# Norm factors of a fused retention and expert kernel: spread over the partitions through DRAM instead of by products with ones

## The chip, the cores and the metric

The kernel runs on one core of a Trainium2 chip. The metric is the device time of one execution in microseconds (us). A core has a matrix engine (PE, TensorE), a vector engine (DVE), a scalar engine (ACT), GpSimd (POOL) and SyncE (SP), which here only issues DMA transfers. Each engine takes its instructions in the order in which they were written, and waits on semaphores for the others.

## What is computed

Three layers follow each other on 2304 tokens (4 batches of 576) of 512 features:

```python
x = retention(q, k, v)                       # per batch and head, with decay
rms = np.sqrt(np.mean(x * x, axis=-1, keepdims=True) + 1e-06)
xn = x / rms * rms_g                         # one factor per token
x = (silu(xn @ w_gate) * (xn @ w_val)) @ w_out
out = sum over 8 experts of P[:, e] * (relu(x @ w1[e]) @ w2[e])
```

The change concerns `1 / rms`, one number per token. The kernel holds x with the features on the partitions and the tokens along the free axis. So a token's factor is needed in all 128 partitions, in the column of that token.

## The kernel before

The program is written with a manual schedule: the order of the Python calls is the order on every engine, and generators (`next(...)`) interleave the pieces of work.

The first stage is the retention loop over `i` in 0 to 15, four head pairs for each of four batches. Step `i` issues on SP the loads of `qT` and `vs` for `i + 2`; then PE makes `scores(i + 1)` (tile `sc`) and `states(i + 1)` (tile `u`), DVE multiplies `sc` by the masks into `am` (L293) and scans the states (L313, L314); SP issues `kT` and `ks` for `i + 3`; and PE makes `outputs(i)` (tile `o`), which DVE scales into `acc` (L342, L344), ACT squares (L349) and POOL adds up over the four pairs of a batch (L351). `sc` and `o` have two buffers each in PSUM; `kT` and `ks` two in SBUF, `qT` and `vs` three, so a load of step `i` waits until PE has read the buffer's last contents. SP issues every load on one queue, in the written order, the weights of the second stage too (`raw`, L109). In the same loop ACT and DVE cut the weights into two parts (L124 to L146).

The norm of batch `b` has two generators. `norm_sums(b)` sums the squares over the partitions by PE (tile `ss`), and makes the factors `r` = `ry`: 128 partitions by 5 columns, token `c * 128 + p` in partition `p`, column `c` (POOL power, then one Newton step on DVE, L385 to L387). `norm(b)` then has to bring them into a row that all partitions hold (tile `y`, 128 x 576), and multiplies x by it, pair by pair (L408); ACT rounds the result into `xhi` (L409), and DVE or POOL takes the rest into `xlo` (L412, L414). The first yields of `norm(b)` are the part that the change replaces: ACT makes five scaled identities `dg` (L395), PE multiplies them by ones into `rb` (L399, L400; the batches 2 and 3 call the second tile `rbt`), ACT copies that into `y` (L402, L403).

For batch 0 this runs in the steps i = 7 to 13 of the retention loop. Batch 1 starts there (i = 13 and 15) and goes on in the first gated block. The second stage is the gated one: six sweeps over five blocks of tokens (`gated_block`, tile `gv` for gate and value, `x` for the output). In the first sweep the norms of the batches 1, 2 and 3 are interleaved with the blocks 0, 1 and 2. The third stage holds the experts, about three quarters of the time, and is not touched.

Of the kernel before, what the change touches and what calls it, by code (L numbers as in the profile page):

```python
# [9 lines left out]
F32 = mybir.dt.float32  # L10
# [7 lines left out]
B, H, S, D = 4, 8, 576, 64  # L18
NP = H // 2
# [6 lines left out]
C = 128  # L26
NC = S // C
TAIL = S - NC * C
# [22 lines left out]
def retention_glu_experts(ctx: ExitStack, tc: tile.TileContext, a, out):  # L51
# [6 lines left out]
    nc = tc.nc  # L58
# [6 lines left out]
    kept = ctx.enter_context(tc.tile_pool(name="kept", bufs=1, space=bass.MemoryType.DRAM))  # L65
# [6 lines left out]
    ident = const.tile([128, 128], F32, name="ident")  # L72
    ones = const.tile([128, 128], F32, name="ones")
# [278 lines left out]
        squares[b] = sq  # L352
        yield

    normed, rstd = set(), {}

    def bank(name):
        pool, tag = ps_home
        return pool.tile([128, 512], F32, tag=tag, name=name)

    def two_banks(b):
        if b < 2:
            t = psa.tile([128, 2, 512], F32, tag="sc", name=f"rb{b}")
            return t[:, 0], t[:, 1]
        return bank(f"rb{b}"), bank(f"rbt{b}")

    def norm_sums(b):

        sq = squares.pop(b)
        if b < B - 1:  # L370
            ss = psa.tile([128, 2, 512], F32, tag="sc", name=f"ss{b}")[:, 0, :NC + 1]
        else:
            ss = bank(f"ss{b}")[:, :NC + 1]
        for c in range(NC + 1):
            w = C if c < NC else TAIL
            nc.tensor.matmul(ss[:w, c:c + 1], lhsT=sq[:, c * C:c * C + w], rhs=ones[:, :1], start=True, stop=True)
        v = nrm.tile([128, NC + 1], F32, tag="rv", name=f"rv{b}")
        r = nrm.tile([128, NC + 1], F32, tag=f"ry{b}", name=f"ry{b}")
        t = nrm.tile([128, NC + 1], F32, tag="rt", name=f"rt{b}")
        nc.vector.memset(v, 1.0)  # L380
        nc.vector.tensor_scalar(v[:, :NC], ss[:, :NC], 1.0 / DM, 1e-6, ALU.mult, ALU.add)
        nc.vector.tensor_scalar(v[:TAIL, NC:], ss[:TAIL, NC:NC + 1], 1.0 / DM, 1e-6, ALU.mult, ALU.add)
        nc.gpsimd.tensor_tensor(out=r, in0=v, in1=mhalf, op=ALU.pow)
        yield
        nc.vector.tensor_mul(t, r, r)  # L385
        nc.vector.scalar_tensor_tensor(t, t, -0.5, v, ALU.mult, ALU.mult)
        nc.vector.scalar_tensor_tensor(r, t, 1.5, r, ALU.add, ALU.mult)  # L387
        rstd[b] = r

    def norm(b):  # L390
        r = rstd.pop(b)
        dg = nrm.tile([128, (NC + 1) * C], F32, tag="dg", name=f"dg{b}")
        dg = dg.rearrange("p (c i) -> p c i", i=C)
        for c in range(NC + 1):
            nc.scalar.mul(dg[:, c, :], ident, r[:, c:c + 1])  # L395
        yield
        rb, rt = two_banks(b)
        rt = rt[:, :TAIL]
        nc.tensor.matmul(rb, lhsT=ones, rhs=dg[:, :NC, :], start=True, stop=True)  # L399
        nc.tensor.matmul(rt, lhsT=ones[:TAIL, :], rhs=dg[:TAIL, NC, :TAIL], start=True, stop=True)  # L400
        y = nrm.tile([128, (NC + 1) * C], F32, tag="dg", name=f"y{b}")[:, :S]
        nc.scalar.copy(y[:, :NC * C], rb)  # L402
        nc.scalar.copy(y[:, NC * C:], rt)  # L403
        yield
        ts = slice(b * S, (b + 1) * S)
        for pr in range(NP):
            x = acc_d[:, pr, ts]
            nc.vector.scalar_tensor_tensor(x, x, rms_g[:, pr:pr + 1], y, ALU.mult, ALU.mult)  # L408
            nc.scalar.copy(xhi[:, pr, ts], x)  # L409
            if pr:  # L410
                p = acc_d[:, pr - 1, ts], f32(xhi[:, pr - 1, ts])
                (nc.vector if pr % 2 else nc.gpsimd).tensor_sub(xlo[:, pr - 1, ts], *p)  # L412
            yield
        nc.vector.tensor_sub(xlo[:, pr, ts], acc_d[:, pr, ts], f32(xhi[:, pr, ts]))  # L414
        normed.add(b)
# [36 lines left out]
    for i in range(B * NP):  # L452
        b, pr = divmod(i, NP)
        load_pair(i + 2, "qT", "vs")
        load_weights(1)
        if i == 2:
            nc.sync.dma_start(rms_g, a["rms_g"])
            nc.sync.dma_start(ident, a["ident"])
            nc.sync.dma_start(wg_raw.rearrange("p k e -> p (k e)"), a["wg"])
        scores(i + 1)  # L460
        states(i + 1)
        load_pair(i + 3, "kT", "ks")
        scale_keys(i + 2)
        out_steps = outputs(i)
        next(out_steps)
        step_weights(load=False, apart=1)
        next(out_steps)
        if i in SUMS_AT:
            next(sums[i // NP - 1], None)
        if i >= 2 * NP - 1:  # L470
            next(norms[0], None)
        if i in (B * NP - 3, B * NP - 1):
            next(norms[1])
    assert 0 in normed
    retention.close()
# [148 lines left out]
    for s in range(NSWEEP):  # L624
        last_sweep = s == NSWEEP - 1
        for j, (t0, n) in enumerate(BLOCKS):
            last = j == len(BLOCKS) - 1
            block = gated_block(s, t0, n, last, pmm, pac, hp, tp, 1 if last_sweep and last else KD, 512)
            first_norms = not s and j + 1 < B
            assert s or (t0 + n - 1) // S in normed  # L630
            for i in range(2 * SWEEP + 1):
                if last_sweep and last and i == 2 * SWEEP:
                    break
                if first_norms and j and not i:
                    next(norms[j + 1])
                if i == 2 * SWEEP:
                    step_weights()
                next(block)
                if first_norms:
                    for _ in range((1, 1, 1, 2, 0)[i]):  # L640
                        next(norms[j + 1], None)
                    if not j and i in (1, 2):
                        next(sums[B - 1], None)
                    if i == 2 * SWEEP - 1 and j + 2 < B:
                        next(norms[j + 2])
                if i == 2 * SWEEP or i < 2 and not first_norms or i == 2 and not s:
                    step_weights()
                if not s and last and not i:
                    nc.scalar.copy(wg[:, :, :E], wg_raw)
                    nc.vector.tensor_sub(wg[:, :, E:], wg_raw, f32(wg[:, :, :E]))  # L650
                if last_sweep and j and i % 2:
                    next(scored)
                if last_sweep and j == 1 and i == 2:
                    load_job(0)
                    load_job2(0)
                if last_sweep and j >= 3:
                    next(first_unit, None)
                    if j == 4:
                        next(first_job, None)
            else:  # L660
                for _ in block:
                    assert 0
# [649 lines left out]
```

## Time and profile before

| what | value |
|---|---|
| time, median of 3 runs (lowest to highest) | 2000.55 us (2000.46 to 2002.4) |
| span of the profiled execution, first to last instruction | 1999.9 us |
| PE busy | 1983.4 us, 99% |
| DVE, ACT, POOL busy | 72%, 43%, 37% |
| granted TensorE clock | 1.000 on average over the span |
| share of the DMA engines in the first 50 us (slice 1 of 40) | 9 tenths |

The span is that of the profiled execution; the median of the timed runs is 0.65 us longer, which is what lies around the span. A share of busy time is an average over stages. PE is busy nearly everywhere; what it waits for in the first 86 us, the retention loop, has to be read there.

### The profile page before, as it was taken

The page shows a single profiled execution, that of the slowest core. Times are in us where ns is not written, and L with a number is a line of the kernel's source. Part 1 is how long each engine was busy: PE and PEld are TensorE (multiplying, and loading weights), DVE is VectorE, ACT ScalarE, POOL GpSimd, SP SyncE. Part 2 cuts the span into 40 slices and gives each one's busy share as a digit, 9 for nine tenths or more (in the row PEclk, how much of TensorE's full clock was granted, in tenths as well). Part 3 has the DMA queues.
Part 4 walks back from the last instruction along what each step waited for, and adds up shares of the span by engine and source line. Part 5 has one row for each costly group of instructions (what it writes and reads, how often), then busy time and mean ns, then how long its engine had stood idle before and what let it go on. Part 6 is the DMA issues. An engine that isn't in the chain of part 4 may idle for free.

```text
span 1999.9 us, 29898 instructions
## 1 busy us (share of the span) xinstructions
PE 1983.4 (99%) x11390; PEld 1856.2 (93%) x11390; DVE 1441.8 (72%) x2276; ACT 869.7 (43%) x1655; POOL 740.4 (37%) x692
## 2 busy tenths in 40 slices
PE   9999999999999999999999999999999999999998
PEld 7788988988889998999999999999999999999998
DVE  6865555554688777777786777777787777777777
ACT  4453323322454444444444444444445444444443
POOL 3300000000153544545544444545466454444543
PEclk9999999999999999999999999999999999999999
DMA  9411111110178888888888676767767767676773
GB/s 314 150 32 53 50 45 52 44 43 1 48 294 301 291 301 305 308 295 311 303 309 313 245 279 239 276 254 263 265 237 282 264 256 280 237 266 251 271 260 142
DMA packets 111535, 436.56 MB, mean 218 GB/s; under 512 B 11720, under 2 KB 29128, under 8 KB 95008
## 3 DMA queue, kind: packets, MB, share of 16 engines
q1 hardware_dynamic: 109904, 432.39, 59.5%
q8 instruction: 89, 1.46, 0.3%
q10 hardware_dynamic: 1248, 1.49, 0.2%
q0 software_dynamic: 240, 0.79, 0.1%
q14 instruction: 54, 0.44, 0.1%
HBM read 312.41 MB, written 122.21 MB: 217 GB/s over the span
## 4 chain that ended last, share of the span: by engine, by line
PE 95%; DVE 3%; DMA 1%; ACT 1%; POOL 0%; issue 0%; ACTq 0%; SPq 0%; DVEq 0%; POOLq 0%
PE py L751 10%; PE pz L751 10%; PE px L751 10%; PE qx L997 7%; PE qy L997 6%; PE qz L997 6%; PE gv L177 5%; PE gv L179 5%; PE gv L178 5%; PE y L178 4%; PE y L179 4%; PE y L177 4%; PE qz L751 3%; PE x L177 2%; PE x L178 2%; PE x L179 2%
## 5 line engine op out<-in xcount | busy, mean ns | idle before, releaser
L751 PE MATMUL py<-sx,w1s 128*128 128x384 f32 x1152 | 232.0, 335 | 1.1 <-ACT py L1089 0.9
L539 POOL TENSOR_TENSOR t<-rw 128x256 f32<-128x256 f32 x32 | 43.0, 1343 | 508.2 <-DVE sx L576 398.8
L1178 POOL TENSOR_TENSOR acc<-z,a_block 128x384 f32<-128x384 f32 x63 | 64.0, 1015 | 434.7 <-DVE z L1172 434.7
L751 PEld LDWEIGHTS py<-sx,w1s 128*128 128x128 f32 x1152 | 203.0, 188 | 5.3 <-ACT py L1089 2.4
L751 PE MATMUL px<-xhi,w1s 128*128 128x384 f32 x640 | 188.8, 335 | 0.3 <-DVE t L205 0.3
L987 ACT CAST xhi<-acc 128x384 fp32r<-128x384 f32 x316 | 156.0, 514 | 69.8 <-POOL acc L1178 35.4
L991 DVE TENSOR_TENSOR xlo<-acc,xhi 128x384 fp32r<-128x384 f32 x191 | 178.3, 960 | 1.8 <-ACT xhi L987 1.8
L991 POOL TENSOR_TENSOR xlo<-acc,xhi 128x384 fp32r<-128x384 f32 x125 | 145.7, 1165 | 29.7 <-ACT xhi L987 29.7
L1005 DVE TENSOR_TENSOR acc<-acc,qz 128x384 f32<-128x384 f32 x246 | 134.9, 548 | 25.5 <-PE qz L997 25.4
L205 DVE TENSOR_TENSOR t<-t,gv 128x512 f32<-128x512 f32 (+1 forms) x60 | 38.0, 633 | 124.6 <-PE gv L179 123.3
L751 PEld LDWEIGHTS px<-xhi,w1s 128*128 128x128 f32 x640 | 117.9, 188 | 0.9 <-DVE t L205 0.6
L1005 DVE TENSOR_TENSOR acc<-acc,qx 128x384 f32<-128x384 f32 x123 | 67.4, 548 | 71.1 <-PE qx L997 71.1
L751 PE MATMUL pz<-sx,w1s 128*128 128x384 f32 x576 | 115.4, 334 | 0.0
L751 PE MATMUL pz<-xhi,w1s 128*128 128x384 f32 x384 | 113.9, 337 | 0.1
L796 DVE SCALAR_TENSOR_TENSOR acc<-y,prob,acc 128x512 f32<-128x512 f32 x144 | 101.4, 742 | 8.1 <-PE y L179 8.1
L751 PE MATMUL px<-xlo,w1s 128*128 128x384 f32 x320 | 107.0, 334 | 0.0
L1023 ACT COPY qz<-qy 128x384 f32<-128x384 f32 x127 | 58.8, 463 | 106.3 <-PE qy L997 100.5
L179 PE MATMUL y<-xlo,xhi 128*128 128x512 f32 x264 | 103.8, 393 | 0.0
L178 PE MATMUL y<-xlo,xhi 128*128 128x512 f32 x264 | 103.6, 393 | 0.0
L177 PE MATMUL y<-xlo,xhi 128*128 128x512 f32 x264 | 102.6, 389 | 0.0
L751 PEld LDWEIGHTS pz<-sx,w1s 128*128 128x128 f32 x576 | 101.3, 188 | 0.7
L1015 ACT COPY qy<-qx 128x384 f32<-128x384 f32 x127 | 58.8, 463 | 95.2 <-PE qx L997 89.4
(401 smaller groups left out, 5890.9 us busy)
## 6 DMA issues: line engine op xcount, KB each, us to landing
w1s<-w_kept SPq DMA_DIRECT2D x64, 1792.0 KB, 7.2
w_kept<-w1s SPq DMA_DIRECT2D x32, 1792.0 KB, 6.6
rw<-in_w_dram SPq DMA_DIRECT2D x64, 512.0 KB, 5.5
w_kept<-xlo SPq DMA_DIRECT2D x64, 512.0 KB, 3.8
w2s<-w_kept SPq DMA_DIRECT2D x32, 1024.0 KB, 6.8
w_extra<-w_kept SPq DMA_DIRECT2D x32, 768.0 KB, 7.7
w_kept<-xlo SPq DMA_DIRECT2D x44, 384.0 KB, 4.3
w2c<-w_kept SPq DMA_DIRECT2D x32, 512.0 KB, 7.9
```

The costliest lines, as they stand in the source:

```text
L177: nc.tensor.matmul(ps, lhsT=lh, rhs=rh, start=start, stop=False)
L178: nc.tensor.matmul(ps, lhsT=lh, rhs=rl, start=False, stop=False)
L179: nc.tensor.matmul(ps, lhsT=ll, rhs=rh, start=False, stop=stop)
L751: nc.tensor.matmul(ps, lhsT=l, rhs=r[:, k, :], start=start and k == 0 and i == 0, stop=k == 1 and i == 2, skip_group_check=True,)
L796: nc.vector.scalar_tensor_tensor(o, y_2, pe, o, ALU.mult, ALU.add)
L987: nc.scalar.copy(hi, x)
L991: (engine or nc.vector).tensor_sub(lo, x, f32(hi))
L997: nc.tensor.matmul(ps, lhsT=l, rhs=r, start=start and i == 0, stop=i == 2, skip_group_check=True)
L1005: nc.vector.tensor_add(dst, dst, ps)
L1015: nc.scalar.copy(y, x)
L1023: nc.scalar.copy(z, y)
L1178: nc.gpsimd.tensor_add(sums[0], z[:, 0, :], h_blocks[0])
```

## The change

The scaled identities, the products with ones and the copies are taken out, with the PSUM tiles that they used (`two_banks`). In their place `norm_sums(b)` ends with a store of `r` from SP into a DRAM tile `rstd_kept[b]`, transposed so that the tokens lie one after the other: 128 partitions x 5 elements of 4 bytes, each with its own address. `norm(b)` begins with a read from SP that gives the same 576 numbers (2304 bytes) to each of the 128 partitions of `y`. `norm(b)` has one yield fewer, so for batch 0, whose first `next` comes at the same step, the multiplications begin one step of the loop earlier; for the other batches one `next` call is taken out, and they stay where they were.

```diff
-    normed, rstd = set(), {}
+    normed = set()
...
-    def two_banks(b):
-        if b < 2:
-            t = psa.tile([128, 2, 512], F32, tag="sc", name=f"rb{b}")
-            return t[:, 0], t[:, 1]
-        return bank(f"rb{b}"), bank(f"rbt{b}")
+    rstd_kept = [kept.tile([NC + 1, C], F32, tag=f"rstd{b}", name=f"rstd_kept{b}") for b in range(B)]
...
         nc.vector.scalar_tensor_tensor(r, t, 1.5, r, ALU.add, ALU.mult)
-        rstd[b] = r
+        nc.sync.dma_start(rstd_kept[b].rearrange("c p -> p c"), r)
 
     def norm(b):
-        r = rstd.pop(b)
-        dg = nrm.tile([128, (NC + 1) * C], F32, tag="dg", name=f"dg{b}")
-        dg = dg.rearrange("p (c i) -> p c i", i=C)
-        for c in range(NC + 1):
-            nc.scalar.mul(dg[:, c, :], ident, r[:, c:c + 1])
-        yield
-        rb, rt = two_banks(b)
-        rt = rt[:, :TAIL]
-        nc.tensor.matmul(rb, lhsT=ones, rhs=dg[:, :NC, :], start=True, stop=True)
-        nc.tensor.matmul(rt, lhsT=ones[:TAIL, :], rhs=dg[:TAIL, NC, :TAIL], start=True, stop=True)
-        y = nrm.tile([128, (NC + 1) * C], F32, tag="dg", name=f"y{b}")[:, :S]
-        nc.scalar.copy(y[:, :NC * C], rb)
-        nc.scalar.copy(y[:, NC * C:], rt)
+        y = nrm.tile([128, S], F32, tag="y", name=f"y{b}")
+        nc.sync.dma_start(y, rstd_kept[b].rearrange("c p -> (c p)")[:S].partition_broadcast(128))
         yield
...
-        if i in (B * NP - 3, B * NP - 1):
+        if i == B * NP - 3:
             next(norms[1])
...
-                if first_norms and j and not i:
-                    next(norms[j + 1])
```

Three places show how the order moves. First SP's queue in the steps i = 6 and 7 of the retention loop; `kT_617` and `ks_619` (`kT_621` and `ks_623` after the change, the numbers are those of buffers) are the loads for pair 9. Before:

```order
L265 DMA kT_617<-in_kT_dram 128x576
L265 DMA ks_619<-in_ks_dram 128x512
L265 DMA qT_653<-in_qT_dram 128x576
L265 DMA vs_655<-in_vs_dram 128x576
L265 DMA kT_682<-in_kT_dram 128x576
L265 DMA ks_684<-in_ks_dram 128x512
L265 DMA qT_723<-in_qT_dram 128x576
L265 DMA vs_725<-in_vs_dram 128x576
```

And now:

```order
L265 DMA kT_621<-in_kT_dram 128x576
L265 DMA ks_623<-in_ks_dram 128x512
L384 DMA rstd_kept_117<-ry_584 128x5x1
L265 DMA qT_658<-in_qT_dram 128x576
L265 DMA vs_660<-in_vs_dram 128x576
L265 DMA kT_687<-in_kT_dram 128x576
L265 DMA ks_689<-in_ks_dram 128x512
L388 DMA y_722<-rstd_kept_117 128x576
L265 DMA qT_724<-in_qT_dram 128x576
L265 DMA vs_726<-in_vs_dram 128x576
```

The store of batch 0's factors stands ahead of the loads of `qT` and `vs` for pair 9, and waits for DVE's last operation on them; the read of `y` stands ahead of the loads for pair 10, and waits until the store has landed. The store of batch 1 stands in the same way between `ks` and `qT` of pair 13.

Second, DVE from the end of step i = 8 (`L344` scales the outputs of pair 8) to the masks of pair 11. Before, L408 is the multiplication by the norm factors:

```order
L344 TENSOR_TENSOR acc<-o_758,g_out 128x512
L293 TENSOR_TENSOR am_797<-sc_796,masks 128x1024
L313 SCALAR_TENSOR_TENSOR block_states_115<-acc,u_795 128x256
L314 SCALAR_TENSOR_TENSOR mt_817<-u_795,tables 128x64
L342 TENSOR_TENSOR acc<-u_727,g_out 128x64
L132 SCALAR_TENSOR_TENSOR cv_644<-raw_513,cv_644 128x512
L344 TENSOR_TENSOR acc<-o_826,g_out 128x512
...
L381 TENSOR_SCALAR rv_859<-ss_853 128x4
L382 TENSOR_SCALAR rv_859<-ss_853 64x1
L408 SCALAR_TENSOR_TENSOR acc<-acc,rms_g,y_788 128x576
L293 TENSOR_TENSOR am_876<-sc_875,masks 128x1024
```

And now, where that line is L393 and L412 is L397:

```order
L344 TENSOR_TENSOR acc<-o_759,g_out 128x512
L393 SCALAR_TENSOR_TENSOR acc<-acc,rms_g,y_722 128x576
L293 TENSOR_TENSOR am_794<-sc_793,masks 128x1024
L313 SCALAR_TENSOR_TENSOR block_states_115<-acc,u_792 128x256
L314 SCALAR_TENSOR_TENSOR mt_814<-u_792,tables 128x64
L342 TENSOR_TENSOR acc<-u_728,g_out 128x64
L132 SCALAR_TENSOR_TENSOR cv_648<-raw_517,cv_648 128x512
L344 TENSOR_TENSOR acc<-o_823,g_out 128x512
...
L378 TENSOR_SCALAR rv_856<-ss_850 64x1
L393 SCALAR_TENSOR_TENSOR acc<-acc,rms_g,y_722 128x576
L397 TENSOR_TENSOR xlo<-acc,xhi 128x576
L293 TENSOR_TENSOR am_874<-sc_873,masks 128x1024
```

One multiplication stands a whole step earlier, ahead of the masks of pair 10, and the second one, with the first `xlo`, stands ahead of the masks of pair 11; the two later steps of batch 0's norm move in the same way, and step 13 has none of it any more.

Third, SP's queue from the last retention loads on (`vs_1073`, after the change `vs_1070`); L109 loads weights. Before:

```order
L265 DMA vs_1073<-in_vs_dram 128x576
L109 DMA raw_1205<-in_gate_dram 128x1024
L109 DMA raw_1398<-in_val_dram 128x1024
L109 DMA raw_1564<-in_gate_dram 128x1024
L109 DMA raw_1665<-in_val_dram 128x1024
```

And now:

```order
L265 DMA vs_1070<-in_vs_dram 128x576
L388 DMA y_1140<-rstd_kept_118 128x576
L384 DMA rstd_kept_119<-ry_1134 128x5x1
L109 DMA raw_1198<-in_gate_dram 128x1024
L384 DMA rstd_kept_120<-ry_1357 128x5x1
L109 DMA raw_1386<-in_val_dram 128x1024
L388 DMA y_1410<-rstd_kept_119 128x576
L388 DMA y_1530<-rstd_kept_120 128x576
L109 DMA raw_1537<-in_gate_dram 128x1024
```

The read for batch 1 stands behind the last load of the retention loop; the reads for the batches 2 and 3 wait for the last multiplication that uses `y` of the batch before, since `y` has one buffer, and weight loads stand behind them.

## Rows read from the trace of the kernel before

**Rows 1.** The page: span, and busy time of each engine (share, instructions).

```profile
span 1999.9 us, 29898 instructions
PE 1983.4 (99%) x11390; PEld 1856.2 (93%) x11390; DVE 1441.8 (72%) x2276; ACT 869.7 (43%) x1655; POOL 740.4 (37%) x692
```

**Rows 2.** Busy time in the gated stage: PE, PEld, DVE, ACT, POOL, clock, DMA share, GB/s.

```profile
85.80:490.00 404.20, 403.94 (x1947) 353.01 (x1946) 220.18 (x373) 136.16 (x252) 8.94 (x6) 1.00 0.14 41
```

**Rows 3.** The chain of waits, 0 to 200 us: start, us on the chain, what.

```profile
45.71 1.09 PE sc L289 x16
...
49.97 1.06 PE rb L399 x2
...
51.38 0.95 PE sc L289 x15
...
82.06 0.45 PE u L326 x4
...
104.47 0.95 PE rb L399 x2
105.41 0.36 PE rbt L400 x2
...
122.33 0.86 PE rb L399 x2
123.18 0.36 PE rbt L400 x2
```

**Rows 4.** Timeline, 48 to 87 us: start, us, engine, line, what [idle before].

```profile
50.29 0.69 DVE L344 TENSOR_TENSOR acc<-o,g_out 128x512 f32<-128x512 f32 x1
52.38 1.22 DVE L293 TENSOR_TENSOR am<-sc,masks 128x1024 f32<-128x1024 f32 x1 [1.41 <-PE sc L289]
...
56.86 0.80 DVE L408 SCALAR_TENSOR_TENSOR acc<-acc,rms_g,y 128x576 f32<-128x576 f32 x1
57.82 1.23 DVE L293 TENSOR_TENSOR am<-sc,masks 128x1024 f32<-128x1024 f32 x1 [0.16 <-PE sc L289]
...
62.13 0.81 DVE L408 SCALAR_TENSOR_TENSOR acc<-acc,rms_g,y 128x576 f32<-128x576 f32 x1
...
62.60 1.61 POOL L351 TENSOR_TENSOR sq<-sq,sq 128x576 f32<-128x576 f32 x1 [2.50 <-ACT sq L349]
...
62.86 1.97 DVE L412 TENSOR_TENSOR xlo<-acc,xhi 128x576 fp32r<-128x576 f32 x1
...
85.06 0.69 DVE L344 TENSOR_TENSOR acc<-o,g_out 128x512 f32<-128x512 f32 x1
...
85.80 0.50 PE L177 MATMUL gv<-xhi,wslots 128*128 128x512 f32 x1
```

**Rows 5.** Timeline, 40 to 45 us: the factors' last step, and two SP issues.

```profile
40.08 0.33 SPq L265 DMA_DIRECT2D qT<-in_qT_dram  x1
...
42.11 0.17 DVE L387 SCALAR_TENSOR_TENSOR ry<-rt,ry 128x5 f32<-128x5 f32 x1
...
44.73 0.33 SPq L265 DMA_DIRECT2D qT<-in_qT_dram  x1
```

**Rows 6.** DMA issues at 38.87, 40.08 and 52.63 us, then `prob_b` (tile): us to landing.

```profile
ks<-in_ks_dram SPq DMA_DIRECT2D x1, 256.0 KB, 5.7
...
qT<-in_qT_dram SPq DMA_DIRECT2D x1, 288.0 KB, 5.3
...
kT<-in_kT_dram SPq DMA_DIRECT2D x1, 288.0 KB, 2.9
...
DMA to landing us min/median/max: 2.5/8.6/9.6
```

**Rows 7.** Timeline, 101 to 108 us: batch 1's last multiplication, batch 2's first.

```profile
101.53 0.81 DVE L408 SCALAR_TENSOR_TENSOR acc<-acc,rms_g,y 128x576 f32<-128x576 f32 x1
...
102.26 0.75 DVE L412 TENSOR_TENSOR xlo<-acc,xhi 128x576 fp32r<-128x576 f32 x1
...
107.65 0.82 DVE L408 SCALAR_TENSOR_TENSOR acc<-acc,rms_g,y 128x576 f32<-128x576 f32 x1 [1.04 <-ACT y L403]
```

## The prediction

> **What bounds the kernel now.** I read the page first: PE is busy for 1983.4 of the span's 1999.9 us [rows 1]. The view by stretches says that the gated stage has no slack at all, with PE busy for 403.94 of 404.20 us [rows 2]. So a PE instruction that is taken out there is time saved, as long as nothing else comes late. The chain of waits names four places where the products with ones are on it: 49.97 us in the retention loop, then just ahead of 85.80, then 104.47 and 122.33 us [rows 3, 4]. The timeline tells what follows each of them. After the first, PE starts the scores of pair 10 at 51.38 instead of 49.97, 1.41 us later, and DVE sits idle for 1.41 us before the masks at 52.38 [rows 3, 4]. From 57.82 us on, DVE works without a pause and PE waits for it; PE takes the last outputs of the loop at 82.06 [rows 3, 4]. The gated stage begins at 85.80, right behind DVE's last scaling of an output (85.06 + 0.69 = 85.75) [rows 4]. PE's products of batch 1, just ahead of it, lie beside that DVE work. So the loop hands over when DVE is done.
>
> **The change, part by part.**
>
> Batches 2 and 3. Their products with ones take 0.95 + 0.36 = 1.31 us and 0.86 + 0.36 = 1.22 us of PE [rows 3], with PE full before and after. Removed: 2.53 us. In their place a read has to land before DVE's first multiplication. For batch 2 it is issued when batch 1's last multiplication ends, 101.53 + 0.81 = 102.34 us; DVE wants it at 107.65 [rows 7], or 1.3 us earlier on the shortened path, about 106.3. That leaves 4.0 us. A load with little ahead of it landed in 2.9 us; a read that likewise gives one row to 128 partitions (`prob_b`) needed 2.5 us at its best and 8.6 in the middle, among heavy traffic [rows 6]. I take 2.9, the nearest in size, and no wait. If it took 8.6 us, DVE would stand 4.6 us ahead of the product of gate and value, which waits for PE anyway. Batch 3 has its read in the same position. Weight loads stand behind these stores and reads on SP, but they are for the second sweep, tens of us later. ACT loses its scalings and copies; it is not on the chain, so I cost that at nothing.
>
> Batch 1. PE's products go, but the hand-over hangs on DVE [rows 4], so this is worth nothing by itself. Its read goes out behind the last retention load, and its use comes only in the first gated block.
>
> Batch 0. PE starts pair 10 at 49.97 us. DVE ends the scaling at 50.29 + 0.69 = 50.98, does the first multiplication, 0.80 us, which now stands here, and takes the masks at 51.8 instead of 52.38. The sums for batch 1 and the operations behind them are released by PE, 1.41 us earlier, so the next multiplication moves from 56.86 to 55.45 and ends at 56.25. Then comes the first `xlo`, formerly in the next step. Its price has two values. Alone it takes 0.75 us [rows 7]; at 62.86 it took 1.97, because POOL had begun an addition at 62.60 and ran to 64.21 [rows 4]. POOL's addition of this step would begin about when `xlo` does, so either can come first. The masks of pair 11 start at 57.0 to 58.2, against 57.82.
>
> From those masks to the gated stage DVE needed 85.80 - 57.82 = 27.98 us [rows 4]. Out of this stretch go the multiplication at 62.13 (0.73 us to the next start) and the `xlo` behind it (1.97) [rows 4], together 2.7; the other four operations of batch 0 move one step inside it. That leaves 25.3 us. The hand-over comes at 57.0 + 25.3 = 82.3 to 83.5, which is 3.5 to 2.3 us earlier; I take the middle, 2.9. PE would be ready sooner: six steps of 49.97 - 45.71 = 4.26 us [rows 3] from 49.97 end at 75.5.
>
> A rule of the Trainium skill bears on that `xlo`. The row shows a DVE operation of 0.75 us held to 1.97, until POOL is done [rows 4, 7]. SBUF — State Buffer, section Who interferes with whom, says that a DVE instruction with two SBUF inputs and a GpSimd instruction that reads SBUF lock one port pair, so that the second to start is blocked for the whole of the first. By that rule the sum has the end 3.5 or the end 2.3, not the middle; the trace agrees with the holding.
>
> What the change adds to SP. The factors are ready at 42.11 + 0.17 = 42.28 us, and the load of `qT` for pair 9, issued at 40.08, now stands behind the store [rows 5]. The store's own issue costs between 0.33 us, as for 128 rows, and five times that, 1.65. So `qT` goes out at 42.6 to 43.9. Before, it landed at 40.08 + 5.3 = 45.4, being queued behind `ks` (38.87 + 5.7 = 44.6) [rows 5, 6], so 0.8 us is one such load's turn. The later issue is then mostly hidden by the queue: 42.6 + 2.9 = 45.5. PE wants it at 45.71 [rows 3]. The store's data were never moved in this way in this trace. Its 640 pieces of 4 bytes cost between nothing (2.5 KB against 288) and five turns of a 128-row load, 5 x 0.8 = 4.0 us. Call that S. At the top `qT` lands at 44.6 + 4.0 + 0.8 = 49.4 and PE stands for 3.7 us. The read of `y` waits on SP for the store's landing, 44.6 + S, and the loads for pair 10 stand behind it (before: 44.73): at S = 0.5 they go out at 45.5 and land by 49.2, wanted at 49.97; `y` lands before its use at 50.98. At the top they are 3.7 us late as well, but PE then is too, so it counts once. Batch 1's store stands in the same way ahead of pair 13's `qT`, where DVE is the bound and PE has slack: 0 to 3.7. By bytes S is near the bottom, by pieces near the top; since PE has 0.2 to 0.8 us of slack here, I take 0.3 us of loss for both stores.
>
> DMA: Bandwidth & Descriptors of the Trainium skill, Rules for kernel authors, speaks against this store: a strided last dimension becomes one descriptor per element, and should be rearranged. No run here shows it yet. Its table of transfers (Bandwidth) has about 10.5 ns per packet; 40 per engine would make S an estimated 0.4 us, and the sum the same as mine.
>
> **Sum.** 2.53 + 2.9 - 0.3 = 5.1 us less. 1999.9 - 5.1 = 1994.8 us of span, and with the 0.65 us by which the median of the runs shown exceeds the span, 1995.4 us.
>
> **Rivals.**
>
> (a) The store stalls the loads in part: S of 1.5 to 2.5, or every `xlo` of batch 0 held by POOL as the one at 62.86 was. For it: the in-order queue, with 0.2 us of slack for pair 9. Against: 2.5 KB. A stall of 1.7 us at both stores gives 1995.1 + 3.4 = 1998.5; two more holds of 1.2 us give 1997.8. Time 1997 to 2000.
>
> (b) Slower: the store's pieces are so dear that SP's queue becomes the bound of the loop. Each store then costs about S, twice on the path. Without the 0.3, the gain is 5.4, so 2S = 5.4, S = 2.7 us, is the point of no change, and S = 4.7 (0.12 us for each of the 40 pieces of an engine) makes the kernel slower by over 0.2%. The top of my bound, 4.0, gives 1995.1 + 7.4 = 2002.5. The same page's Specifications section speaks of a read-modify-write below 512 B, which would be such a price; no run here shows it.
>
> (c) Faster still: no `xlo` is held, 3.5 instead of 2.9, no loss on SP, and one more hold of 1.2 us, that POOL's work of batch 0 makes today, goes away: 2.53 + 3.5 + 1.2 = 7.2, 1993.3 us.
>
> (d) The loop keeps its length, since DVE's work stays the same in sum: only batches 2 and 3 gain, 1998.0. Against: the idle 1.41 us before the masks [rows 4], which the moved operations fill.
>
> **Chances.** Forecast, 1994.2 to 1996.5: 0.60. (a) with (d), 1997 to 2000: 0.22. (c): 0.11. (b): 0.07. A measurement of this kernel can tell about 0.2%, 4.0 us, from no change, so faster ends at 1996.5: the forecast and (c) make 0.71, (a) and (d) 0.22, (b) 0.07. For 8 in 10 the range goes from 1993.3, all of (c), to 1998.6, about half of (a) and (d).
>
> **What would show it.** Right: no products with ones on PE; PE passing from `x` to `gv` without a gap at the blocks 1 and 2; DVE's masks of pair 10 close to 51.8 us; `gv` starting at 82.3 to 83.5, directly behind the scaling of the last output. Wrong: PE waiting for the `qT` of pair 9, 10 or 13; the store landing over 3 us after its issue; DVE waiting for `y` of batch 0 after 51 us; a `gv` that starts at 85 or later.

## The result: 1.1% slower, and the profile after

The changed kernel took 2023.38 us (median of 4 runs, 2022.89 to 2024.13) against 2000.86 us for the kernel before (4 runs, 2000.46 to 2002.4): a ratio of 1.0111, 95% interval 1.0099 to 1.0124. The forecast was 1995.4 us.

The page of the profiled execution, first lines (they answer to [rows 1]):

```profile
span 2021.1 us, 29856 instructions
PE 1983.5 (98%) x11374; PEld 1857.9 (92%) x11374; DVE 1441.5 (71%) x2276; ACT 861.6 (43%) x1627; POOL 744.8 (37%) x692
```

PE has 16 instructions fewer and is busy for the same 1983.5 us, though 2.53 us of products went out with the batches 2 and 3 alone. So PE waits longer, and some of its products run slower. The waits of PE from 0 to 130 us (engine, line, what it waits for: us in total, times, longest):

```profile
PE sc L289 <- DMA qT<-in_qT_dram: 22.8, 4, 10.2
PE gv L177 <- DVE acc L344: 2.1, 1, 2.1
```

Of the 22.8 us, 2.3 lie in the first 30 us, where no norm is at work yet. The kernel before waits for `qT` for 2.5 us there and for 0.3 us from 30 to 130 us, so the change brings about 20 us of such waits. The chain of waits from 40 to 126 us says where; it answers to [rows 3]:

```profile
42.60 12.34 DMA qT<-in_qT_dram
54.98 2.08 PE sc L289 x16
...
72.76 12.15 DMA qT<-in_qT_dram
85.05 2.08 PE sc L289 x16
...
105.25 0.50 PE gv L177
...
123.47 10.34 DMA y<-rstd_kept
```

Two loads of `qT`, for the pairs 9 and 13, are on the chain for 12 us each. Each was issued right behind a store of norm factors. The scores of pair 9 begin at 54.98 instead of 45.71 us, 9.3 later, and the gate products at 105.25 instead of 85.80, 19.4 later. A third long transfer, of 10.34 us, stands on the chain in the gated stage: batch 2's read, issued at 123.47, behind batch 3's store at 120.16. It makes PE wait for 1.6 us only (for `ghi`, L206). The DMA issues at 41.72 and 72.29 us, with the time from issue to landing at the end of each row, show the cause at its source:

```profile
rstd_kept<-ry SPq DMA_DIRECT2D x1, 2.5 KB, 10.3
...
rstd_kept<-ry SPq DMA_DIRECT2D x1, 2.5 KB, 11.3
```

2.5 KB need 10.3 and 11.3 us. SP's own issue took only 0.38 us. From 44 to 52 us the DMA engines count as busy for three quarters of the time and move 24 to 29 GB/s, against 221 and 313 GB/s in the rows behind; the last row lies behind batch 2's store, issued at 102.09, and looks alike. The view by stretches (PE, PEld, DVE, ACT, POOL, granted clock, DMA share, GB/s):

```profile
44.00:48.00 4.00, 0.74 (x14) 0.49 (x10) 1.71 (x4) 1.26 (x2) 1.40 (x1) 1.00 0.75 24
48.00:52.00 4.00, 0.00 (x0) 0.00 (x0) 0.00 (x0) 0.00 (x0) 0.00 (x0) 0.57 0.74 29
52.00:56.00 4.00, 1.02 (x9) 1.02 (x10) 0.00 (x0) 0.00 (x0) 0.00 (x0) 0.50 0.76 221
56.00:60.00 4.00, 4.00 (x54) 3.42 (x54) 2.66 (x6) 1.43 (x3) 0.00 (x0) 0.65 0.90 313
...
105.00:112.00 7.00, 6.75 (x22) 5.38 (x23) 0.92 (x2) 2.10 (x4) 1.43 (x1) 0.76 0.90 27
```

The rows show a second price. PE stands still from 48 to 52 us, and its granted clock falls to 0.50, the level of 1.2 GHz; the scores that follow take 2.08 us instead of 1.09 [rows 3]. At the hand-over to the gated stage PE waits for 2.1 us, and the clock is 0.76 in the 7 us behind it.

The hand-over itself, in the timeline from 102 to 106 us (start, us, engine, line):

```profile
102.44 1.60 POOL L351 TENSOR_TENSOR sq<-sq,sq 128x576 f32<-128x576 f32 x1 [2.39 <-ACT sq L349]
...
102.71 1.89 DVE L132 SCALAR_TENSOR_TENSOR cv<-raw,cv 128x512 int32<-128x512 int32 x1
104.52 0.68 DVE L344 TENSOR_TENSOR acc<-o,g_out 128x512 f32<-128x512 f32 x1
...
105.25 0.50 PE L177 MATMUL gv<-xhi,wslots 128*128 128x512 f32 x1 [2.12 <-DVE acc L344]
```

L132, an operation on weights that took 0.68 us at 99.77, takes 1.89 here, beside POOL's addition, which ends at 104.04. The last scaling L344 stands behind it, and PE behind that.

### The profile page after: what moved, and what is told of

It is laid out like the page before. It is cut to its first block, busy times and chain, and to the rows that moved or that the text cites. A ratio compares the mean times of both kernels' runs of the same rounds, so it can differ in the third digit from the quotient of the medians.

```text
span 2021.1 us, 29856 instructions
## 1 busy us (share of the span) xinstructions
PE 1983.5 (98%) x11374; PEld 1857.9 (92%) x11374; DVE 1441.5 (71%) x2276; ACT 861.6 (43%) x1627; POOL 744.8 (37%) x692
## 4 chain that ended last, share of the span: by engine, by line
PE 94%; DMA 3%; DVE 2%; ACT 1%; issue 0%; POOL 0%; SPq 0%; ACTq 0%; DVEq 0%
PE pz L734 10%; PE py L734 10%; PE px L734 10%; PE qx L980 6%; PE qy L980 6%; PE qz L980 6%; PE gv L177 5%; PE gv L179 5%; PE gv L178 5%; PE y L178 4%; PE y L179 4%; PE y L177 4%; PE qz L734 3%; PE x L177 2%; PE x L178 2%; PE x L179 2%
```

## The experiments

Three theories of the store's price were to be told apart: the count of 640 pieces; the smallness of a piece; and that pieces of 4 bytes which lie next to each other in DRAM hold each other up. Beside them stood SP's order: the store waits for its data, the read for the store's landing, and the loads queue behind both.

**1. The store alone, and everything but the store.** `store_only` is the kernel before with the four stores added, which nothing reads. `read_only` is the changed kernel without them; its reads take a constant row.

```diff
 # store_only, on the kernel before
         nc.vector.scalar_tensor_tensor(r, t, 1.5, r, ALU.add, ALU.mult)
+        nc.sync.dma_start(rstd_kept[b].rearrange("c p -> p c"), r)
         rstd[b] = r
```
```diff
 # read_only, on the changed kernel
-        nc.sync.dma_start(rstd_kept[b].rearrange("c p -> p c"), r)
...
-        nc.sync.dma_start(y, rstd_kept[b].rearrange("c p -> (c p)")[:S].partition_broadcast(128))
+        nc.sync.dma_start(y, a["g_out"].rearrange("p n -> (p n)")[:S].partition_broadcast(128))
```

> The kernel before, with products and copies kept, and the four stores added at the places where the change has them; nothing reads them. Theory 1: the loads for pair 9 and pair 13 are 10 us late as in the changed kernel, each with about 2 us more for PE at half its clock, 2020 to 2027 us. Theory 2: only the issue of qT moves by 2 to 3 us, under 2005 us.

> The changed kernel without its four stores; the broadcast read takes a constant row of an input, so the norm factors are left out of the result. Theory 1 (the store's 640 small pieces fill the queue for 10 us): without them the rest of my sum holds, 1993 to 1998 us, no wait of PE for qT over 1 us, gated stage reached at 82 to 84 us. Theory 2 (the order of SP's queue does it: the read, and what it and the loads wait for): still above 2010 us.

`store_only` took 2021.32 us, ratio 1.0102 (1.0082 to 1.0122); its stores landed after 9.3 to 11.5 us. `read_only` took 1998.47 us, ratio 0.9986 (0.9976 to 0.9995), with 0.9 us of waits for `qT` from 30 to 130 us and the gate products at 84.15; both time and start are a little above what was expected. So the store, at its place in SP's queue, makes most of the loss even where nothing reads it, 20.2 us of 22.5, and the rest of the change gains 2.7 us where the prediction had 5.4 without its 0.3 for SP. The two don't add up to the whole (20.2 less 2.7 is 17.5): some 5 us appear only where a store and a read that waits for it come together, and no run takes them apart. The row of `read_only` that matters later, from the view by stretches:

```profile
85.00:90.00 5.00, 5.00 (x13) 3.89 (x13) 0.00 (x0) 0.32 (x1) 1.37 (x1) 0.50 0.23 85
```

**2. What about the store is dear.** Four kernels change the pieces. `spread` and `spread64` keep the 640 pieces of 4 bytes but put them 512 and 64 bytes apart; `wide` has 512 pieces of 512 bytes; `rows20` has 128 packed pieces of 20 bytes.

```diff
 # spread (spread64: one tile for each batch, and 16 instead of 128)
+    spread = kept.tile([(NC + 1) * C, 128], F32, tag="rstd", name="rstd_kept")
...
-        nc.sync.dma_start(rstd_kept[b].rearrange("c p -> p c"), r)
+        nc.sync.dma_start(rstd_kept[b].rearrange("(c p) w -> p c w", p=C)[:, :, 0], r)
...
```
```diff
 # wide: the factors stand in column 0 of a tile of ones, 128 x 4 x 128
+        nc.sync.dma_start(rstd_kept[b].rearrange("(c p) w -> p c w", p=C), wide)
...
 # rows20
+        nc.sync.dma_start(rstd_kept[b].rearrange("c p -> (c p)").rearrange("(p c) -> p c", c=NC + 1), r)
```

> The changed kernel with each 4-byte piece stored 512 bytes from the next; the read takes 576 numbers in a row, so the factors are wrong. If the price is the count of pieces (theory 1), landing stays at 9 to 11 us and the time at 2018 to 2028 us. If neighbours of 4 bytes fight for the same line of DRAM (theory 1b), landing falls to 2.5 to 5 us and the time under 2003 us.

> The changed kernel with 512 pieces of 512 bytes instead of 640 of 4, in the same place; the read takes 576 numbers in a row, so the factors are wrong. If the price is the count of pieces, landing at 7 to 9 us and 2012 to 2022 us. If it is their smallness (theory 1c), the 256 KB land in 2.5 to 4.5 us like a load, and the time is under 2003 us.

> The store writes the same 2560 bytes as the changed kernel's, but as 128 pieces of 20 bytes, one for each partition, packed one behind the other (so the factors stand in the wrong order in y; the work and its order are the changed kernel's otherwise). If it is the count of pieces that costs, the store lands in about a fifth of the 10 us, 2 to 3 us, and the time is near that of the kernel before. If pieces of under 512 bytes that lie next to each other hold each other up, one piece in five is left, so the same 2 to 3 us come out of it; the two then differ only by the run whose 640 pieces lie 512 bytes apart, which landed in about 3 us. If a partly written stretch of memory costs the same however many pieces fall into it, it stays at 8 us or more, for the stretch of 2560 bytes is the same.

> The changed kernel with its 640 pieces of 4 bytes 64 bytes apart in DRAM, not 4 and not 512 (its DRAM tile is filled once at the start by four small loads, so that no part of it is unset). If pieces hold each other up because they fall into one 64-byte stretch, this is as good as 512 bytes apart: the store lands in about 3 us and the time is near 2005 to 2008 us. If the stretch is larger than 64 bytes, the store lands in between, 4 to 9 us, and the time is 2009 to 2019 us. If it is the count of pieces, it lands in 10 us.

The pages of the profile count the pieces as packets: the changed kernel has 2048 more than `rows20`, four times 640 less 128, and `spread` has the changed kernel's number but for 10. The view of the store's line, with its issues and the landing times, in `spread`:

```profile
L385 SPq DMA_DIRECT2D rstd_kept<-ry x4: 371/377/381, 45.7 to 109.8; - x4
...
DMA to landing us min/median/max: 2.4/2.7/3.0
```

The same view of `spread64`:

```profile
L384 SPq DMA_DIRECT2D rstd_kept<-ry x4: 371/377/381, 46.0 to 106.3; - x4
...
DMA to landing us min/median/max: 2.4/2.5/3.1
```

Of `wide`:

```profile
L386 SPq DMA_DIRECT2D rstd_kept<-wide x4: 370/378/381, 42.0 to 101.9; - x4
...
DMA to landing us min/median/max: 2.4/2.5/3.5
```

And of `rows20`:

```profile
L384 SPq DMA_DIRECT2D rstd_kept<-ry x4: 319/327/330, 42.9 to 103.6; - x4
...
DMA to landing us min/median/max: 1.4/1.4/2.9
```

The same 640 pieces of 4 bytes land in 2.4 to 3.1 us when they are 64 bytes apart, in 9.4 to 11.3 when they are 4 bytes apart. Neither the count nor the size of a piece does that by itself; what differs is the distance to the neighbour, and 64 bytes are enough. `rows20` writes the same packed 2560 bytes in 1.4 to 2.9 us, so a dense stretch as such is not dear, only many pieces in it. How the chip comes to it, and at which distance below 64 bytes it begins, wasn't tried.

The times are 2007.07 us for `spread` (ratio 1.0027, 1.0012 to 1.0042) and 2002.38 for `wide` (1.0007, 0.9997 to 1.0017); `spread64` and `rows20` ran once each, with 2005.84 and 2004.17 us, so they have no interval. `spread` stands above the 2003 that was expected with a cheap store: PE still waits for `qT`, from 30 to 130 us for 6.7 us in `spread` and 5.4 in `wide` (20.5 in the changed kernel, 0.9 in `read_only`). That rest was put down to SP's order, and the third group tests it.

**3. A cheap store, and SP's order.** `turned` has a store of 128 pieces of 128 bytes: DVE turns the factors in blocks of 32 x 32. `ordered` moves this store behind the `qT` and `vs` of its step, and batch 0's read behind the next step's.

```diff
 # turned, on the changed kernel
...
+        wide = nrm.tile([128, 32], F32, tag="ry", name=f"ry{b}")
+        turned = nrm.tile([128, 32], F32, tag="turned", name=f"turned{b}")
+        r = wide[:, :NC + 1]
+        nc.gpsimd.memset(wide, 1.0)
...
-        nc.sync.dma_start(rstd_kept[b].rearrange("c p -> p c"), r)
+        nc.vector.transpose(turned, wide)
+        nc.sync.dma_start(rstd_kept[b].rearrange("c (k p) -> k c p", p=32), turned)
```
```diff
 # ordered, on turned
         nc.vector.transpose(turned, wide)
+        yield
...
         load_weights(1)
+        if i >= NP and i % NP == 3:
+            next(sums[i // NP - 1], None)
+        if i == 2 * NP:
+            next(norms[0])
...
-        if i >= 2 * NP - 1:
+        if i >= 2 * NP:
             next(norms[0], None)
...
-                    if not j and i in (1, 2):
+                    if not j and i in (1, 2, 3):
                         next(sums[B - 1], None)
```

> The whole computation, with the store mended: DVE turns the 128 x 5 factors in blocks of 32 x 32, so that the store has 128 pieces of 128 bytes, each a row of the DRAM tile; the read is the changed kernel's. The theory that neighbouring pieces of 4 bytes are the whole trouble: the store lands in 2 to 3 us after its issue, PE's waits for qT in the retention loop fall from 22.8 to 3 to 7 us, and the time to 1998 to 2003 us. The rival, SP's order (a store that waits for r and a read that waits for the landing hold the loads behind them): the time stays above 2008.

> The whole computation, with the turned store (128 pieces of 128 bytes) one place later in SP's queue, behind the qT and vs of its step, and the read of batch 0 behind the next step's qT and vs; the multiplications stand where the changed kernel has them. Theory that SP's order is what is left of the loss in the turned version (7.1 us of waits for qT): these waits fall below 2 us, the gate products start at 83.5 to 85 us with a wait of 2 to 3 us for DVE's L344 ahead of them, and the time is 1998 to 1999.5. Rival, that stores and reads cost the DMA engines themselves so much that the loads are late in any order: the waits stay at 5 us or more and the time at 2003 to 2005.

`turned` took 2004.78 us, ratio 1.0018 (1.0009 to 1.0028); `ordered` took 2000.63 us, 0.9999 (0.9989 to 1.0008). DVE's turning took 0.21 us. The trace gives no landing of the turned stores; SP issued batch 0's read, which waits for it, 3.2 us behind the store (41.73 and 44.96), where the changed kernel had 10.4 (41.72 and 52.07). The waits of PE in `turned`, 30 to 130 us:

```profile
PE sc L289 <- DMA qT<-in_qT_dram: 7.1, 4, 2.6
PE gv L177 <- DVE acc L344: 2.3, 1, 2.3
```

and in `ordered`, 35 to 90 us:

```profile
PE gv L177 <- DVE acc L344: 3.4, 1, 3.4
PE u L292 <- DVE acc L342: 1.1, 2, 0.7
PE sc L289 <- DMA qT<-in_qT_dram: 0.3, 1, 0.3
```

By the ratios, the turned store takes back 18.6 us of the loss (1.0111 less 1.0018, of 2001); `spread`, which changes nothing of the store but the distance, takes back 16.8 (1.0111 less 1.0027). The new order gains another 3.8 (1.0018 less 0.9999). That figure is rough, since each ratio is known to about 2 us; `wide`, whose store lands as soon and stands in the old order, has 1.0007. Behind both stands no loss any more, but no gain either. `turned` lies between the two theories (up to 2003, and above 2008), since both were at work; `ordered` came out 1 us above its 1998 to 1999.5, with the waits for `qT` gone as expected and the gate products at 85.36, later than expected. A store on another engine's queue was not tried.

**4. Where the gain of the hand-over went.** `late` gives only the batches 2 and 3 the turned store and the read, and leaves the products to the batches 0 and 1. `read_busy` and `ordered_busy` give PE 12 products that nothing uses, ahead of the first gate product. `read_ahead`, `ahead` and `before_ahead` exchange two things in the last step of the loop, on `read_only`, `ordered` and the kernel before: the last scaling L344 goes ahead of the two operations on weights.

```diff
 # read_busy, ordered_busy
+    idle_ps = bank("idle_ps2")
+    keep_busy(12)
     assert 0 in normed
```
```diff
 # read_ahead, ahead, before_ahead
+        last_pair = i == B * NP - 1
+        if last_pair:
+            next(out_steps)
         step_weights(load=False, apart=1)
-        next(out_steps)
+        if not last_pair:
+            next(out_steps)
```

> The whole computation. Batches 0 and 1, whose norms stand in the retention loop, keep the products with ones; the batches 2 and 3 go through DRAM with the store that DVE turns. The prediction's term for those two, 2.53 us of PE, taken alone: if it is right, PE goes from block to block without a wait for y and the time is 1998.0 to 1998.8 (ratio 0.9987). If the store and the read are late or take DMA from the weights, PE waits for DVE's L408 or xhi in the blocks 1 and 2, and the time is that of the kernel before or above.

> The kernel with the reads alone (constant factors, the norm factors are left out), plus 12 products of 128 x 512 on PE between the last outputs of the retention loop and the first gate product, which nothing uses. In the kernel with the reads alone PE waits there for 3.14 us, its granted clock then stands below 1.00, and the first gate products take 0.80 us instead of 0.50. Theory that the lost clock eats half of the gain of the shorter loop: with PE kept busy the stretch from 85 to 130 us has a clock of 0.99 to 1.00 and the time falls by 2 to 3 us, to about 1996 (ratio 0.9965 to 0.998). Rival, that the loop gives no more than those 1.65 us whatever the clock: the time stays at 1998 to 1999.

> The version before, plus the 12 products on PE that nothing uses, ahead of the first gate product. If the clock that is lost in the wait ahead of the gate products is worth 2 to 3 us there as it was in the kernel with the reads alone, this is 1996 to 1998 us (ratio 0.997 to 0.9985), the sum of the prediction after all but 1 to 2 us. If the loop still waits for loads, PE is idle elsewhere, the clock falls there, and the time stays at 1999 or above.

> The kernel with the reads alone (constant factors, the norm factors are left out), with one thing exchanged in the last step of the retention loop: DVE scales the last outputs (L344) ahead of its two operations on weights (L146, L132), not behind them. In the kernel with the reads alone the L132 there was held to 1.89 us by POOL's addition, and L344 came only then. Theory that this hold and the clock behind it are the missing part of the hand-over's term: L344 starts at about 81.0 us, the gate products at 81.7 to 82.0 and at full clock, and the time is 1994 to 1996 us (ratio 0.9965 to 0.9975). Rival, that DVE's work as a whole bounds the hand-over and that the weights are then late in the first block: the gate products start early, but PE waits in the block for the pieces of weights, and the time stays at 1998.

> The whole computation: the turned store in its later place in SP's queue, and DVE's last L344 ahead of the two operations on weights. In the version without that exchange L344 started at 84.62 and the gate products at 85.36, after a wait of 3.35 us in which POOL held L146 to 1.87 us. Expected: gate products at 82.8 to 83.3, a wait there of about 1 us, granted clock back at 0.99 to 1.00 between 85 and 130 us, and a time of 1996 to 1998 us (ratio 0.9975 to 0.9985), the best of the complete kernels. By the rival the time stays at 2000.

> The kernel before, with that exchange alone, to see what of it is owed to the change. There L344 starts at 85.06 behind L146 (83.86) and L132 (84.45), none of them held. Expected: L344 starts at about 83.9 and the gate products up to 1.2 us earlier; PE's products for batch 1 stand ahead of them and keep the clock. Time 1999.5 to 2001 (ratio 0.9992 to 1.0000). A gain of 2 us or more would say that the exchange has nothing to do with the hold.

| kernel | us, median | ratio (95% interval) | wait of `gv` for L344, us |
|---|---|---|---|
| `late` | 2000.12 | 0.9995 (0.9986 to 1.0003) | 1.4 |
| `read_only` | 1998.47 | 0.9986 (0.9976 to 0.9995) | 3.1 |
| `read_busy` | 1997.18 | 0.9977 (0.9968 to 0.9986) | 0.5 |
| `ordered` | 2000.63 | 0.9999 (0.9989 to 1.0008) | 3.4 |
| `ordered_busy` | 1998.59 | 0.9987 (0.9979 to 0.9996) | 0.7 |
| `read_ahead` | 1995.89 | 0.9971 (0.9960 to 0.9982) | 0.8 |
| `ahead` | 1996.62 | 0.9972 (0.9963 to 0.9981) | 0.9 |
| `before_ahead` | 2001.91 | 1.0002 (0.9993 to 1.0010) | none |

The timeline of `ordered` at the hand-over, DVE, POOL and PE:

```profile
82.16 1.40 POOL L351 TENSOR_TENSOR sq<-sq,sq 128x576 f32<-128x576 f32 x1 [0.80 <-ACT sq L349]
82.23 1.87 DVE L146 TENSOR_TENSOR wslots<-cv,wslots 128x512 fp32r<-128x512 f32 x1
...
84.02 0.68 DVE L132 SCALAR_TENSOR_TENSOR cv<-raw,cv 128x512 int32<-128x512 int32 x1
84.62 0.68 DVE L344 TENSOR_TENSOR acc<-o,g_out 128x512 f32<-128x512 f32 x1
...
85.36 0.50 PE L177 MATMUL gv<-xhi,wslots 128*128 128x512 f32 x1 [3.35 <-DVE acc L344]
```

and of `ahead`:

```profile
84.33 1.41 POOL L351 TENSOR_TENSOR sq<-sq,sq 128x576 f32<-128x576 f32 x1 [0.80 <-ACT sq L349]
84.40 0.68 DVE L344 TENSOR_TENSOR acc<-o,g_out 128x512 f32<-128x512 f32 x1
...
85.00 1.28 DVE L146 TENSOR_TENSOR wslots<-cv,wslots 128x512 fp32r<-128x512 f32 x1
...
85.13 0.50 PE L177 MATMUL gv<-xhi,wslots 128*128 128x512 f32 x1 [0.90 <-DVE acc L344]
```

In `ordered` L146 takes 1.87 us beside POOL's addition, which ends at 83.56, and L344 and PE stand behind it. In `ahead` L344 passes in 0.68 us beside the same POOL addition, and L146 is held behind it, where PE doesn't wait for it. PE's wait shrinks by 2.45 us (3.35 to 0.90). The hold is 1.2 of them; the rest is the two operations' own time, which no longer stands ahead of L344. (The last steps of this execution of `ahead` lie some 2 us later, so the gate products missed the 82.8 to 83.3 that was expected. The first loads came about 1 us late, and PE waited 1.2 us for a `qT` at 71. The time in the table is that of 11 runs.) The exchange does nothing for the kernel before: there the products of batch 1 keep PE busy until `gv`, which started at 86.32, not up to 1.2 us earlier as expected. So its gain belongs to the changed program, and `ahead` beats the kernel before by 0.28% (0.19 to 0.37), 5.6 us. That is about what the prediction summed up for the change as it stood, but it confirms nothing of that sum, since it takes another store, another order and the exchange. `ahead` came out better than expected (0.9975 to 0.9985), `read_ahead` as expected, and `ordered_busy`, with 0.9987, just outside its 0.9970 to 0.9985.

`late` missed its 1998.0 to 1998.8. It has the hold as well: there L132 took 1.89 us, where in the kernel before it began 0.12 us ahead of POOL's addition and took 0.69. DVE's turning, 0.2 us more ahead of it, was enough to lose that. The lost 1.2 us, and a gain of 2.53, would make 1.3; `late` gained 1.0 us, with an interval that takes in no gain at all.

`read_busy` shows the clock's part. By the ratios it is about 1.8 us better than `read_only` (0.0009 of 2001), though the intervals overlap; `ordered_busy` stands 2.4 us below `ordered` (0.0012), and its interval excludes the kernel before. The stretch from 85 to 90 us of `read_busy` reads

```profile
85.00:90.00 5.00, 5.00 (x28) 4.24 (x26) 0.61 (x1) 1.16 (x2) 0.74 (x1) 1.00 0.14 53
```

The clock is 1.00 here and 0.50 in `read_only`, both with PE busy for the whole 5 us. 18 of these 28 are gate products, which start 0.23 us apart, and ten are short sums (`ss`, L371); the 13 of `read_only` are gate products 0.43 us apart. These rows are of one execution each, and that of `read_only` (2000.0 us) was slower than its median. `read_ahead` is 3.0 us better than `read_only` (0.0015): it takes away the hold and keeps the clock, and the runs don't tell the two apart.

## Why the prediction was wrong

**The step that failed** is the price of the store, S: how long its data hold the loads behind it on SP's queue. The text had bounded it by "nothing (2.5 KB against 288) and five turns of a 128-row load, 5 x 0.8 = 4.0 us", and taken 0.5. It measured 10.3 and 11.3 us in the retention loop. The bound came from rows of another kind of transfer, loads with long pieces; no row of the kernel before had neighbouring pieces of 4 bytes, so it bounded nothing, and the 0.3 us for both stores, which rested on it, was off by 20: PE waited 20.5 us for the two loads. Pieces set 64 bytes apart, 2.5 us, would have stood inside it. VectorE: DVE Perf Modes of the Trainium skill, The three transpose paths, warns of a transposition by the strides of a plain DMA copy when the innermost stride of the destination is large. The prediction didn't draw on it. It would have spoken against this store, but a large stride is not what costs here: by the tiles' shapes that stride is 512 bytes in the changed kernel and 8192 in `spread64`, which landed in 2.5 us. The faster DMA path that the section names was not tried here.

**Rival (b) named the mechanism**, SP's queue as the bound of the loop, with 0.07. By its own sum, 1995.1 + 2S, the two measured prices give 1995.1 + 10.3 + 11.3 = 2016.7 us. For the other 6.7 us up to 2023.4 the profile has these: batch 2's read behind batch 3's store, after which PE waits 1.6 us for `ghi` (L206); about 1.7 us of clock in the 7 us from 105 on (7 x 0.24); L132's hold of 1.2; and the scores at 2.08 us, twice 1.0 too long. That makes 6.5, a rough account from single rows, whose close agreement is partly chance: the products behind those scores were slow as well. A firmer reading needs no sum: against the profile of `read_only` the gate products stand 21.1 us later (105.25 and 84.15), with 20.5 us of waits for `qT` where `read_only` has 0.9.

The Trainium skill was cited on both sides of S. DMA: Bandwidth & Descriptors, Rules for kernel authors, said to rearrange such a store, and the runs agree. The estimate of 0.4 us, from the 10.5 ns per packet in its Bandwidth section, does not hold here: 10.3 us for 40 pieces per DMA engine are 0.26 us a piece, and the measurement decides. The page's figure is that of loads, 0.67 us over 64 packets; taken over all 640 pieces it would be an estimated 6.7 us, which the 2.5 us of `spread64` contradicts too. Nor is it the read-modify-write below 512 bytes of its Specifications section by size alone: pieces of 4 bytes, 64 bytes apart, landed as fast as pieces of 512. Whether such writes hold each other up when they fall close together is open.

**Batches 2 and 3** were right in mechanism as far as seen: the products are out, and in `ahead` PE waits for nothing longer than 0.2 us between the first gate product and 160 us. The size of 2.53 us isn't shown in a time: `late`, which was to take it alone, lost a part to the hold and can't be told from no gain. In the changed kernel itself batch 2's read took 10.3 us instead of 2.9, because it stands behind batch 3's store.

**Batch 0** was right in mechanism. In `read_only` the masks of pair 10 start at 51.42 us (predicted 51.8) and those of pair 11 at 57.31 (57.0 to 58.2), and `xlo` takes 0.74, not held. The gate products came at 84.15, 1.65 us earlier instead of 2.9. The missing 1.2 us are one hold by POOL: the prediction had looked for it at `xlo`, and it came at L132. In the kernel before, L132 had begun 0.12 us ahead of POOL's addition:

```profile
84.35 1.13 PE L399 MATMUL rb<-dg,ones 128*128 128x512 f32 x2
84.45 0.69 DVE L132 SCALAR_TENSOR_TENSOR cv<-raw,cv 128x512 int32<-128x512 int32 x1
84.57 1.85 POOL L351 TENSOR_TENSOR sq<-sq,sq 128x576 f32<-128x576 f32 x1 [2.02 <-ACT sq L349]
...
85.41 0.43 PE L400 MATMUL rb<-dg,ones 64*128 64x64 f32 x2
```

In `read_only` it began 0.45 us behind the addition's start, after DVE had stood idle for 0.47 us until POOL's power (L378):

```profile
80.39 0.17 DVE L380 TENSOR_TENSOR rt<-ry 128x5 f32<-128x5 f32 x1 [0.47 <-POOL ry L378]
...
81.16 1.79 POOL L351 TENSOR_TENSOR sq<-sq,sq 128x576 f32<-128x576 f32 x1 [0.80 <-ACT sq L349]
81.61 1.89 DVE L132 SCALAR_TENSOR_TENSOR cv<-raw,cv 128x512 int32<-128x512 int32 x1
83.42 0.68 DVE L344 TENSOR_TENSOR acc<-o,g_out 128x512 f32<-128x512 f32 x1
...
84.15 0.80 PE L177 MATMUL gv<-xhi,wslots 128*128 128x512 f32 x1 [3.14 <-DVE acc L344]
```

Without the hold `gv` would stand at an estimated 82.95, in the predicted 82.3 to 83.5. The port rule that the prediction quoted from the Trainium skill (SBUF — State Buffer, Who interferes with whom) agrees with these rows; the prediction applied it to one place only.

**Batch 1** was costed at "nothing by itself", and that was wrong by about 2 us, as far as the runs with added products (`read_busy`, `ordered_busy`) tell. Its products, L399 and L400 in the rows of the kernel before, were what kept PE busy from 84.35 us up to the gate products at 85.80. With them gone PE waits there for 2.1 to 3.4 us in the versions without added products or the exchange. In the profile of `read_only`, where it waits for 3.1, the clock is 0.50 from 85 to 90 us.

**SP's order** was a term of 0.3 us for both stores; even with a cheap store it is about 3.8 us, the difference of `turned` and `ordered`, each known to about 2 us. The prediction let the `qT` of pair 9 hide in the queue, and added nothing up over the loads behind a store that waits for its data and a read that waits for the store.

**The 0.65 us** by which the median exceeds the profiled span is not what lies around the span, as the section on the time before has it. Every timed run listed is 1.7 to 1.9 us longer than its own span (2022.89 and 2021.1 for the changed kernel), so the profiled execution was itself, by an estimate from these, about 1.1 us slower than the median. The sum isn't touched, since it comes to the median less 5.1.

## What to carry to other kernels

A transfer of a few KB need not be cheap because it is small: look at how far apart its pieces land, and if they are many neighbours of 4 bytes, as here, turn the data first (0.21 us on DVE) so that each piece is a row. A store that waits for an engine, and a read that waits for the store, belong behind the loads that are wanted soon. Before work is taken off an engine ahead of a hand-over, see whether it was what kept that engine's clock up, and which other instruction comes to stand beside one that holds it up when everything moves by a few tenths of a microsecond.

## What the runs showed of the hardware

- 640 pieces of 4 bytes from 128 partitions to DRAM: 9.3 to 11.5 us to land when neighbours are 4 bytes apart, 2.4 to 3.1 us at 64 or 512 bytes. The `qT` loads issued right behind the packed store in the changed kernel stand on the chain for 12.3 and 12.2 us.
- Where PE had waited for 3.1 us ahead of the gate products (`read_only`), the granted clock from 85 to 90 us was 0.50, the level of 1.2 GHz, with PE busy throughout. Behind waits of 0.5 to 1.4 us (`read_busy`, `ordered_busy`, `read_ahead`, `ahead`, `late`) it stayed at 1.00. In `ordered`, behind a wait of 3.4 us, the first gate products still took their usual time, and then the sixth 0.53 and the seventh 0.63 us instead of 0.39: the clock fell when PE was at work again. Waits in between went both ways: 1.00 from 91 to 98 us in `turned` behind 2.3 us, 0.76 in the changed kernel behind 2.1.
- DVE's L344, which has one input in PSUM and one in SBUF, was not held by the POOL addition that held L132 and L146, whose inputs are all in SBUF (0.68 against 1.87 to 1.89 us).
